# Two transpositions moved ahead of loads on the DMA queue of an attention and MLP kernel

## The chip, the cores and the metric

The kernel runs on one core of a Trainium2 chip. The metric is device time in microseconds, the median of several runs of the whole kernel. TensorE, VectorE, ScalarE and GpSimd compute; SyncE (SP in the profile) issues the DMAs.

## What is computed

The reference is a linear attention with decay, followed by an MLP with a tanh GELU. Cut to what matters:

```python
# q, k, v: (4, 8, 768, 64); lam: (8,); blocks of 64 positions
intra = einsum('bhic,bhjc->bhij', qb, kb) * Dmask        # lam ** (i - j), causal
intra = einsum('bhij,bhjd->bhid', intra, vb)
inter = einsum('bhid,bhde->bhie', qb * lam_pow, kv_state)
out[block] = intra + inter
kv_state = lam_block * kv_state + einsum('bhsd,bhse->bhde', kb * rev_pow, vb)
# then, on x of shape (3072, 512):
h = x @ w_in                                             # (512, 2048)
g = 0.5 * h * (1 + tanh(c * (h + 0.044715 * h**3)))
return g @ w_out                                         # (2048, 512)
```

## The kernel before

**Steps.** The attention is cut into 24 steps. One step is a block of 256 positions of one batch, for four of the eight heads; two steps make the 256 rows of `x` that belong to one block. For each step three loads of 256 KB are issued, q, k and v, by `load_step` (line 70). Their tiles `q32`, `k32` and `v32` come from a pool with four buffers each.

**Preparation of a step.** `prep_qk(s)` does two things. `cast_qk` makes a float16 tile `qk16` of both: VectorE multiplies q by a decay (`cast_q`, line 282), ScalarE copies k (`cast_k`, line 295). Then `transpose_dma` (line 303) has the DMA engines transpose that tile into `qkT`, for steps 8 and later; the instruction is issued by SP and waits for both casts. `scale_v` (line 266) has GpSimd scale v.

**Attention of a step.** `scores` (line 350) are TensorE's products of keys and queries, read out of `qkT`, into two PSUM banks `S`. `causal` (line 360) has VectorE multiply them by the mask into `PT`. `products` gives a step's output in two banks `OK`. From step 13 on, steps go in pairs through `burst`: all scores of two newer steps, then the outputs `O` of older steps (line 460, two banks), then the state products `K` of the newer steps (line 475, two banks), then the rest of `O` (lines 488 and 498); ScalarE copies the outputs to `xT` (lines 527 and 529).

**The MLP as filler.** The rows that the attention has finished go through the MLP in pieces, kept in a list `filler`; `fill(n)` emits the next n of them between the parts of the attention. A piece of the first product fills one PSUM bank `Hps` with four matmuls (line 613), and ScalarE applies the GELU from it (line 617). Pieces of the second product (line 692) come after these.

**PSUM.** All tiles in PSUM come from one pool of eight banks, which are handed out in turn. A tile can be written when the engine that empties the tile of eight allocations before has done so. Around the change TensorE's order of new banks is: six `Hps` (between 81.6 and 86.9 us), four `S` of steps 13 and 14, two `O`, two `K`, then `Hps` again.

**Order.** Nothing is scheduled: `pin` keeps every instruction in the order in which the program writes it, on its engine. So the order of SP's DMAs is that of the calls `load_step`, `transpose_dma` and the stores. Around the change it is, in the loop over n = 11 and 12 and after it:

```
n = 11: transposition of 13, v of 14, q and k of 16
n = 12: transposition of 14, transposition of 15, v of 15, v of 16
after:  q and k of 17, transposition of 16, v of 17, two stores
```

The matching orders on the other engines are, for ScalarE: cast of k of step 15, three GELUs, cast of k of step 16, three GELUs, copies of `O`; for VectorE: cast of q of 15, a sum of weights (line 151), cast of q of 16, the masks of steps 13 and 14. TensorE has the six `Hps`, then `burst((13, 14), (12,))`, six more `Hps`, and `burst((15, 16), (13, 14))`.

Of the kernel before, what the change touches and what calls it, by code (L numbers as in the profile page):

```python
# [15 lines left out]
def kernel(  # L16
# [43 lines left out]
    def load_step(s, names="qkv"):  # L60
        b, r = divmod(s, 2 * NSB)
        sb, half = divmod(r, 2)
        ts = ld32.setdefault(s, [])
        for nm, src in (("q", q), ("k", k), ("v", v)):
            if nm not in names:
                continue
            t = ld.tile([P, HH, 2, D], FP32, tag=nm + "32", name=f"{nm}32_{s}")
            rows = src[b, half * HH : (half + 1) * HH, sb * SB : (sb + 1) * SB, :]
            queue = nc.scalar if (nm, s) == ("v", 0) else nc.sync
            pin(queue.dma_start(out=t[:].rearrange("p h j d -> p h (j d)"),  # L70
                                in_=rows.rearrange("h (p j) d -> p h (j d)", j=2)))
            ts.append(t)
# [191 lines left out]
    def scale_v(s):  # L264
        tv = a16p.tile([P, 2, HH, D], FP16, tag="v16", name=f"v16_{s}")
        pin(nc.gpsimd.tensor_tensor(wide(tv[:]), ld32[s][2][:], decay(dv, s), ALU.mult))  # L266
        a16[s] = a16[s] + (tv,)

    def prep_qk(s):
        cast_qk(s)  # L270
        transpose_dma(s)

    def cast_qk(s):
        cast_q(s)
        cast_k(s)

    def cast_q(s):
        q32 = ld32[s][0]
        tqk = a16p.tile([P, 2, 2, HH, D], FP16, tag="qk16", name=f"qk16_{s}")
        tq, tk = tqk[:, 0], tqk[:, 1]  # L280
        q_eng = nc.gpsimd if s == 3 else nc.vector
        pin(q_eng.tensor_tensor(wide(tq), q32[:], decay(dq, s), ALU.mult))  # L282
        if s == 0:
            inverse(halves[0])
            odd(halves[1])
            inverse(halves[1])
        a16[s] = (tq, tk)
        whole_qk[s] = tqk

    def cast_k(s):  # L290
        tk, k32 = a16[s][1], ld32[s][1]
        if s == 4:
            pin(nc.vector.tensor_copy(out=wide(tk), in_=k32[:]))
        else:
            pin(nc.scalar.activation(out=wide(tk), in_=k32[:], func=AF.Copy))  # L295
# [3 lines left out]
    def transpose_dma(s):  # L299
        tqk = whole_qk.pop(s)  # L300
        if s >= FIRST_DMA_T:
            o = qkp.tile([P, 2, 2, 2, P], FP16, tag="qkT", name=f"qkT_{s}")
            pin(nc.sync.dma_start_transpose(out=o[:].rearrange("p a j h t -> p (a j h) t"),
                                            in_=tqk[:].rearrange("p a j h d -> p (a j h d)")))
            qkT[s] = o
            if s == FIRST_DMA_T + 1:
                load_step(s + 1, "v")

    def stage_t(s):
        if s >= FIRST_DMA_T:  # L310
            return
        tq, tk = a16[s][:2]
        if s < 4:
            Tps = [ps_M.tile([P, 2, 2, P], FP16, tag="M", name=f"Tps{i}") for i in range(2)]
        else:
            Tps = ps_M.tile([P, 2, 2, 2, P], FP16, tag="M", name="Tps")
        for i, t in enumerate((tq, tk)):
            to = Tps[i] if s < 4 else Tps[:, i]
            for hp in range(2):
                for j in range(2):  # L320
                    pin(nc.tensor.transpose(to[:, j, hp, :], t[:, j, 2 * hp : 2 * hp + 2, :],  # L321
                                            ident[:]))
        o = qkp.tile([P, 2, 2, 2, P], FP16, tag="qkT", name=f"qkT_{s}")
        if s < 4:
            pin(nc.scalar.activation(out=o[:, 0], in_=Tps[0][:], func=AF.Copy))
            pin(nc.vector.tensor_copy(out=o[:, 1], in_=Tps[1][:]))
        elif s in (5, 6, 8):
            pin(nc.scalar.activation(out=o[:], in_=Tps[:], func=AF.Copy))
        else:
            pin(nc.vector.tensor_copy(out=o[:], in_=Tps[:]))  # L330
        qkT[s] = o
# [203 lines left out]
    def update(s, c, parts="tu"):  # L535


        sbg, half = divmod(s, 2)
        sb = sbg % NSB
        if c == 1 and sb == NSB - 1:  # L540
            Kps.pop(s)
            return
        if "t" in parts:
            K = (Kps[s] if c == 0 else Kps.pop(s))[c].rearrange("p (hp d) -> p hp d", hp=2)
            t = ucp.tile([P, 2, D], FP32, tag=f"t{half}", name=f"t_{s}_{c}")
            if sb == 0 and c == 0:
                pin(nc.vector.tensor_copy(out=t[:], in_=K))
            else:
                for hp in range(2):
                    pin(nc.vector.scalar_tensor_tensor(  # L550
                        t[:, hp, :], state[half][:, hp, :],
                        lamu[:, 2 * half + hp : 2 * half + hp + 1], K[:, hp, :],
                        ALU.mult, ALU.add))
            state[half] = t
        if "u" in parts:
            if (s if c == 0 else s + 2) in NARROW:
                u = ubp.tile([P, 2, 2, D], FP16, tag=f"u{half}", name=f"u_{s}_{c}")[:, 0]
                pin(nc.gpsimd.tensor_tensor(  # L558
                    u, state[half][:],
                    lamu[:, 2 * half : 2 * half + 2].unsqueeze(2).to_broadcast([P, 2, D]),  # L560
                    ALU.mult))
                us[(s, c)] = u
                return
            u = ubp.tile([P, 2, 2, D], FP16, tag=f"u{half}", name=f"u_{s}_{c}")
            pin(nc.gpsimd.tensor_tensor(  # L565
                u[:], state[half][:].unsqueeze(2).to_broadcast([P, 2, 2, D]),
                lumask[:, 2 * half : 2 * half + 2, :].unsqueeze(3).to_broadcast([P, 2, 2, D]),
                ALU.mult))
            us[(s, c)] = u
# [21 lines left out]
    def store_pair(pair):  # L591
        rows = out[2 * pair * P : 2 * pair * P + 2 * P, :].rearrange("(i p) d -> p i d", p=P)
        for i in range(2):
            pin(nc.sync.dma_start(out=rows[:, i], in_=o_pairs[pair][:, i]))
# [363 lines left out]
    def fill(n):  # L958
        for _ in range(min(n, len(filler))):
            filler.pop(0)()  # L960

    def R(n, s, ahead=None, keep=False):

        def first():
            if n is not None:
                scores(n)
            if ahead:
                ahead()

        if s in NARROW:  # L970
            products(n, s, between=first)
        else:
            first()
            products(n, s)
        if n is not None:
            causal(n)
        if s is not None and s % 2 == 1:
            g, i = group_of[s // 2]
            if i == len(groups[g]) - 1 and g > 0:
                queue_group(g)  # L980
        if n is not None and not keep:
            update(n, 0)

    def U(n):
        update(n, 1)
# [98 lines left out]
    for n, (a, b, c, d) in FILL.items():  # L1084
        stage_t(n)
        fill(a + (n == 10))
        if n == 8:
            cast_q(n + 2)
            fill(1)
            cast_k(n + 2)  # L1090
            transpose_dma(n + 2)
        else:
            prep_qk(n + 2)
        if n < 11:
            load_step(n + 4, "qkv" if n < 10 else "qk")
        if n == 9:
            store_pair(1)
        if n == 11:
            scale_v(13)
            load_step(14, "v")  # L1100
            load_step(16, "qk")
        elif n == 9:
            scale_v(11)
        elif n == 10:
            scale_v(12)
            load_step(15, "qk")
        elif n == 12:
            scale_v(14)
        fill(b + (n == 8) - (n == 10))
        R(n, n - 1, keep=n == 8)  # L1110
        fill(c)
        if n == 8:
            update(n, 0)
            scale_v(n + 2)
            fill(2)
        U(n)
        if n == 12:
            prep_qk(15)
            load_step(15, "v")
            load_step(16, "v")  # L1120
            scale_v(15)
        fill(d)
        if n > 8:
            sum_win((n - 7) // 2, (n - 1) % 2, nc.vector)

    cast_qk(16)
    load_step(17, "qk")
    transpose_dma(16)
    load_step(17, "v")
    while kept_stores:  # L1130
        kept_stores.pop(0)()
    scale_v(16)
# [86 lines left out]
```

## Time and profile before

| | |
|---|---|
| median of 3 runs | 198.23 us (198.18 to 198.6) |
| the profiled execution's own time | 198.31 us |
| its span | 196.5 us |
| TensorE matmul busy | 189.7 us (97%) |
| VectorE, ScalarE, GpSimd busy | 145.7, 126.0, 68.1 us |
| DMA queue of SP | 62240 packets, 37.50 MB |
| granted TensorE clock | full nearly throughout (mean 0.997) |

The span is the time from the first to the last instruction that the profiler recorded on the core; the run's time has 1.8 us around it. Busy times are sums over instructions; a matmul's end is modelled, so TensorE's busy share does not say how near it is to its peak. In a timeline each row is a start in us, a length in us, the engine and line, the operation, the tiles, how many were merged, and in brackets the idle time ahead of it with what ended it. SPq is SP's issuing of DMAs: its rows tell when a DMA was issued, not when its data arrived. The landing comes from the DMA view, as the time from the start of the issue to the last completion mark.

### The profile page before, as it was taken

The numbers are of one execution on the slowest core, as the hardware profiler recorded it, in microseconds if no ns is written. First come the engines' busy times: TensorE is split into PE (matmuls) and PEld (weight loads), VectorE is DVE, ScalarE is ACT, GpSimd is POOL, SyncE is SP. The second block draws the span as 40 slices with busy tenths as digits, with TensorE's granted clock in tenths as the row PEclk, the third lists the DMA queues.
The fourth block names the chain that finished last, engine by engine and source line by source line (L and its number), as shares of the span: only waits on it lengthen the run. The fifth ranks groups of instructions, "written<-read, shape, count | busy, mean of one in ns | idle before, by whom it ended". The sixth has DMA issues, their size and how long they took to land.

```text
span 196.5 us, 5992 instructions
## 1 busy us (share of the span) xinstructions
PE 189.7 (97%) x2469; PEld 138.7 (71%) x2469; DVE 145.7 (74%) x291; ACT 126.0 (64%) x250; POOL 68.1 (35%) x85
## 2 busy tenths in 40 slices
PE   8878999999999999999999999999999999999992
PEld 2546544456888888654688754578888888888882
DVE  4987732889989879949889926999557996487520
ACT  3673778357774796686856379844877856678211
POOL 6594213557444732068524416064002030002000
PEclk9999999999999999999999999999999999999998
DMA  6999999999999999999997999600520300021105
GB/s 168 291 322 385 386 386 387 298 286 295 255 218 237 262 343 219 213 217 302 256 275 169 266 307 156 146 4 0 47 87 29 110 5 0 3 107 45 65 29 184
DMA packets 62810, 38.13 MB, mean 194 GB/s; under 512 B 18624, under 2 KB 55744, under 8 KB 62784
## 3 DMA queue, kind: packets, MB, share of 16 engines
q1 hardware_dynamic: 62240, 37.50, 76.8%
q8 instruction: 19, 0.31, 0.7%
q10 hardware_dynamic: 544, 0.26, 0.5%
q14 instruction: 7, 0.06, 0.1%
HBM read 27.26 MB, written 6.29 MB: 171 GB/s over the span
## 4 chain that ended last, share of the span: by engine, by line
PE 89%; SPq 4%; DMA 4%; ACT 0%; issue 0%
PE Hps L613 25%; PE MX L692 18%; PE MY L692 9%; PE HX L791 7%; PE O2ps L628 7%; PE MW L692 4%; DMA wi<-in_moe_w_in_dram 4%; SPq L70 4%; PE HY L791 4%; PE S L350 3%; PE Hps L890 3%; PE HW L791 2%; PE O L460 1%; PE OK L400 1%; PE Tps L321 1%; PE OK L422 1%
## 5 line engine op out<-in xcount | busy, mean ns | idle before, releaser
L613 PE MATMUL Hps<-xT,w_in 128*128 128x512 f16 (+1 forms) x288 | 50.5, 332 | 0.0
L613 PEld LDWEIGHTS <-w_in 128*128 128x128 f16 x288 | 27.8, 98 | 19.4
L617 ACT ACTIVATE gT<-Hps 128x512 f16<-128x512 f32 x56 | 32.6, 597 | 9.1 <-PE Hps L613 8.7
L360 DVE TENSOR_TENSOR PT<-S,mask 128x512 f16<-128x512 f32 x48 | 30.3, 680 | 8.6 <-PE S L350 8.6
L692 PEld LDWEIGHTS <-gs 128*128 128x128 f16 x320 | 31.1, 98 | 3.7
L266 POOL TENSOR_TENSOR v<-v,dv 128x512 f16<-128x512 f32 x24 | 27.5, 1150 | 17.3 <-DMA v<-in_v_dram 17.1
L692 PEld LDWEIGHTS <-gT 128*128 128x128 f16 x240 | 23.2, 98 | 3.5 <-ACT gT L617 0.2
L565 POOL TENSOR_TENSOR u<-t,lumask 128x256 f16<-128x256 f32 x21 | 15.2, 737 | 22.6 <-DVE t L550 13.6
L692 PE MATMUL MX<-w_sum,gs 128*128 128x256 f16 x160 | 21.4, 273 | 0.0
L662 DVE TENSOR_TENSOR gs<-gT 128x1024 f16<-128x1024 f16 (+1 forms) x24 | 17.2, 722 | 3.0 <-ACT gT L617 3.0
L282 DVE TENSOR_TENSOR qk<-q,dq 128x512 f16<-128x512 f32 x23 | 18.3, 798 | 1.2 <-DMA q<-in_q_dram 1.1
L295 ACT ACTIVATE qk<-k 128x512 f16<-128x512 f32 x23 | 14.4, 625 | 7.2 <-DMA k<-in_k_dram 7.1
L744 POOL TENSOR_TENSOR o<-u,q 128x512 f32<-128x512 f32 (+1 forms) x5 | 6.1, 1212 | 37.0 <-ACT u L709 37.0
L558 POOL TENSOR_TENSOR u<-t,lamu 128x128 f16<-128x128 f32 x19 | 10.7, 572 | 21.3 <-DVE t L550 15.7
L628 PE MATMUL O2ps<-w_out,gT 128*128 128x512 f16 x64 | 14.6, 379 | 0.0
L791 PEld LDWEIGHTS <-ws 128*128 128x128 f16 x128 | 12.4, 98 | 1.6 <-DVE xs L770 0.2
L529 ACT ACTIVATE xT<-OK 128x256 f16<-128x256 f32 x22 | 8.7, 453 | 6.7 <-PE OK L422 3.1
L709 ACT ACTIVATE u<-MX 128x256 f32<-128x256 f32 x18 | 6.9, 383 | 7.4 <-PE MX L692 7.4
L628 PEld LDWEIGHTS <-gT 128*128 128x128 f16 x64 | 6.1, 98 | 6.6
L692 PE MATMUL MY<-w_out,gs 128*128 128x256 f16 x80 | 10.7, 273 | 0.0
L805 DVE COPY u<-HX 128x512 f32<-128x512 f32 x8 | 5.5, 689 | 6.8 <-ACT gT L809 4.4
L692 PE MATMUL MX<-w_sum,gT 128*128 128x256 f16 x80 | 10.4, 273 | 0.0
(105 smaller groups left out, 322.0 us busy)
## 6 DMA issues: line engine op xcount, KB each, us to landing
q<-in_q_dram SPq DMA_DIRECT2D x24, 256.0 KB, 5.0
k<-in_k_dram SPq DMA_DIRECT2D x24, 256.0 KB, 5.1
v<-in_v_dram SPq DMA_DIRECT2D x23, 256.0 KB, 5.2
out_dram<-o SPq DMA_DIRECT2D x23, 256.0 KB, 4.1
wo<-in_moe_w_out_dram SPq DMA_DIRECT2D x4, 1024.0 KB, 9.5
wi<-in_moe_w_in_dram SPq DMA_DIRECT2D x4, 512.0 KB, 8.2
wi<-in_moe_w_in_dram SPq DMA_DIRECT2D x2, 1024.0 KB, 12.8
v<-in_v_dram ACTq DMA_DIRECT2D x1, 256.0 KB, 4.3
```

Of the source, the lines that this page charges most:

```text
L266: pin(nc.gpsimd.tensor_tensor(wide(tv[:]), ld32[s][2][:], decay(dv, s), ALU.mult))
L282: pin(q_eng.tensor_tensor(wide(tq), q32[:], decay(dq, s), ALU.mult))
L295: pin(nc.scalar.activation(out=wide(tk), in_=k32[:], func=AF.Copy))
L360: pin(nc.vector.tensor_tensor(t[:, hl].rearrange("p b c d -> p b (c d)"), Sps[:].rearrange("p b c d -> p b (c d)"), mask[:].unsqueeze(1).t ...
L558: pin(nc.gpsimd.tensor_tensor(u, state[half][:], lamu[:, 2 * half : 2 * half + 2].unsqueeze(2).to_broadcast([P, 2, D]), ALU.mult))
L565: pin(nc.gpsimd.tensor_tensor(u[:], state[half][:].unsqueeze(2).to_broadcast([P, 2, 2, D]), lumask[:, 2 * half : 2 * half + 2, :].unsqueez ...
L613: pin(nc.tensor.matmul(by_block(Hps[:, i, :]), w_in16[:, c, f * P : (f + 1) * P], x(c), start=(c == 0), stop=(c == NC - 1)))
L617: pin(nc.scalar.activation(out=dst, in_=Hps[:], func=AF.Gelu_apprx_tanh))
L628: pin(nc.tensor.matmul(O2[tau][0][:], gT[:, f % HF, f // HF, tau * P : (tau + 1) * P], w_out16[:, f, :], start=(n == 0), stop=(n == NF - 1)))
L662: pin(nc.vector.tensor_tensor(g_rows(m, i), g_rows(a, i), g_rows(b, i), op))
L692: pin(nc.tensor.matmul(dst, lhsT, rhs, start=(opens and i == 0), stop=(closes and i == HF - 1), skip_group_check=True))
L791: pin(nc.tensor.matmul(dst[:, i, :], w_in_block(a, slice(c, c + 1), slice(f * P, f * P + P))[:, 0], x_block(b, slice(c, c + 1))[:, 0], sta ...
```

## The change

At two places a transposition is issued ahead of two loads that stood ahead of it. The loads of q and k of step 16 go from n = 11 to n = 12, behind the transposition of step 14. The loads of q and k of step 17 go behind the transposition of step 16; there the separate calls become `prep_qk(16)` and `load_step(17)`, which issue the same instructions. The number of instructions does not change, nor does the order on TensorE, VectorE, ScalarE and GpSimd, nor the PSUM banks.

```diff
             prep_qk(n + 2)
         if n < 11:
             load_step(n + 4, "qkv" if n < 10 else "qk")
+        elif n == 12:
+            load_step(16, "qk")
         if n == 9:
             store_pair(1)
         if n == 11:
             scale_v(13)
             load_step(14, "v")
-            load_step(16, "qk")
         elif n == 9:
             scale_v(11)
...
-    cast_qk(16)
-    load_step(17, "qk")
-    transpose_dma(16)
-    load_step(17, "v")
+    prep_qk(16)
+    load_step(17)
     while kept_stores:
         kept_stores.pop(0)()
     scale_v(16)
```

SP's order after the change:

```
n = 11: transposition of 13, v of 14
n = 12: transposition of 14, q and k of 16, transposition of 15, v of 15, v of 16
after:  transposition of 16, q, k and v of 17, two stores
```

## Prediction

> **What bounds the kernel now.** I read the page first. Its chain of work that ended last is nearly all TensorE:
>
> ```profile
> PE 89%; SPq 4%; DMA 4%; ACT 0%; issue 0%
> ```
>
> From about 20 us to 193 us the chain is TensorE without a break, so an earlier transfer gains only where TensorE waited for it, and any new TensorE wait goes whole into the end. The change sits between 80 and 94 us. The chain there, in order of time (start, us, what):
>
> ```profile
> 81.80 5.18 PE Hps L613 x24
> 86.98 0.67 PE S L350 x32
> 87.88 0.28 PE K L475 x32
> ...
> 93.56 0.57 PE S L350 x32
> ```
>
> These are the two bursts: scores of steps 13 and 14 at 86.98, of 15 and 16 at 93.56. The same 32 matmuls take 0.67 us in the first and 0.57 in the second. So at most 0.10 us at step 14's scores can be a wait for its transposition. That is all the first move can give back.
>
> The order in time on the DMA queue (SP: start, us to issue):
>
> ```profile
> 79.47 0.58 SPq L70 DMA_DIRECT2D v<-in_v_dram  x1
> 80.10 0.51 SPq L70 DMA_DIRECT2D q<-in_q_dram  x1
> 80.65 0.55 SPq L70 DMA_DIRECT2D k<-in_k_dram  x1
> 81.36 3.32 SPq L303 DMA_TRANSPOSE qkT<-qk  x2
> 84.73 1.93 SPq L70 DMA_DIRECT2D v<-in_v_dram  x2
> 86.71 0.51 SPq L70 DMA_DIRECT2D q<-in_q_dram  x1
> 87.26 0.51 SPq L70 DMA_DIRECT2D k<-in_k_dram  x1
> 87.93 1.85 SPq L303 DMA_TRANSPOSE qkT<-qk  x1
> ```
>
> 80.10 and 80.65 are q and k of step 16, 81.36 the transpositions of 14 and 15, 86.71 and 87.26 q and k of step 17, 87.93 the transposition of 16. Asked for the loads issued from 80.65, the DMA view gives the landing:
>
> ```profile
> k<-in_k_dram SPq DMA_DIRECT2D x1, 256.0 KB, 4.4
> ```
>
> 80.65 + 4.4 is 85.0. Who takes it, in the timelines of VectorE, ScalarE and TensorE:
>
> ```profile
> 84.18 0.86 DVE L282 TENSOR_TENSOR qk<-q,dq 128x512 f16<-128x512 f32 x1 [0.59 <-DMA q<-in_q_dram]
> ```
> ```profile
> 84.43 0.60 ACT L617 ACTIVATE gT<-Hps 128x512 f16<-128x512 f32 x1 [0.27 <-PE Hps L613]
> 85.03 0.63 ACT L295 ACTIVATE qk<-k 128x512 f16<-128x512 f32 x1
> 85.57 1.19 ACT L617 ACTIVATE gT<-Hps 128x512 f16<-128x512 f32 x2
> 87.02 0.60 ACT L617 ACTIVATE gT<-Hps 128x512 f16<-128x512 f32 x1 [0.27 <-PE Hps L613]
> ```
> ```profile
> 87.48 0.39 PE L460 MATMUL O<-PT,v 64*64 64x128 f16 x16
> 87.71 0.45 PE L475 MATMUL K<-v,qk 64*64 64x64 f16 x32
> ```
>
> VectorE already waits 0.59 us for q of step 16. ScalarE takes k of step 16 at 85.03, in the very moment it lands: no slack. Behind it stand three GELUs. PSUM's eight banks go round in order of allocation, so the second `O` bank needs the fourth `Hps` bank of this run emptied, the first `K` bank the fifth, the second `K` bank the sixth. The sixth GELU ends at 87.02 + 0.60 = 87.62, TensorE wants that bank at about 87.73: slack 0.1 us.
>
> [...] The trace agrees with the order: v of 14 lands 3.8 us after 79.47, at 83.3, q of 16 at 84.2, k at 85.0. [...] The trace has one such packet at 85.25, 996 ns long, on the instruction queue.
>
> That fetch matters. The windows (us; five engines busy; clock, DMA share, GB/s) show full flow, then almost none:
>
> ```profile
> 81.25:85.50 4.25, 4.25 (x24) 2.09 (x22) 3.07 (x7) 3.50 (x8) 2.07 (x2) 1.00 1.25 295
> 85.75:87.00 1.25, 1.25 (x12) 0.47 (x14) 0.00 (x0) 0.99 (x2) 0.81 (x2) 1.00 0.05 6
> ```
>
> [...] The semaphore of the DMA just ahead of that transposition is held too: the transposition of 14 finished its packets by 85.5, yet fifteen of its sixteen marks came at 87.10 to 87.19. The same happened one fetch earlier: k of 15, issued at 75.33, took 6.2 us, where k of 16 took 4.4.
>
> **The change part by part.** No instruction is added or removed. The engines' own orders, their waits for PSUM and the banks stay; SP's order alone changes, at two places.
>
> Transposition of 14 ahead of q and k of 16. On SP it goes past two loads (0.51 + 0.55 us). Its casts were done by 79.8 (VectorE: 79.08 + 0.68), so it can start at 80.10 instead of 81.36 and lands near 84.2. Gain at TensorE: at most 0.10 us, and that only brings TensorE sooner to banks that ScalarE has not emptied; I take 0.
>
> q and k of 16 slip behind it: on SP by its issue time, 1.7 us (half of 3.32), in the DMA engines by 256 KB, 0.9 us at 295 GB/s. The flow is full, so the 0.9 counts first: k of 16 ends its packets where the transposition of 14 did, about 85.4 instead of 84.4, directly ahead of the transposition of 15. Lower bound of its landing L: 85.03 + 0.9 = 85.9. If held as its predecessor in that place was: 87.1. I take 87.1, since fetch, place and following transposition are the same.
>
> What waits: ScalarE stands at the cast from 85.03 to L. Then cast to next GELU 0.54 (85.57 - 85.03), two GELUs 1.19, the last 0.59: the sixth bank is free at L + 2.32, and with 0.06 for the signal TensorE's second `K` bank starts at L + 2.38 instead of 87.73. TensorE's new wait is **L - 85.35**. With 87.1 it is 1.75 us, with 85.9 0.55. It begins at the `O` matmuls (87.48) and all later TensorE work follows behind it, with no idle time to take it up. VectorE's cast of q, at worst 87.2 to 88.0, delays step 13's mask by 0.6; its result is first read in the next burst, at 94: nothing.
>
> Transposition of 16 ahead of q and k of 17. It needs the cast of k of 16: 87.1 + 0.63 = 87.7, so it issues near 87.8, as before (87.93), and lands near 92.5; step 16's scores come at 93.8 + 1.75. Gain 0. q and k of 17 go out near 89.7 and 90.2, 3 us later, and land near 93.9 and 94.7. Their casts stood at 92.53 (VectorE) and 94.09 (ScalarE). Behind the first is the mask of step 15, whose scores now come after 95.3; behind the second the copies of `O`, now near 96.9. Both covered by 0.5 us or more; if that cover fails, a few tenths. v of 17 and the stores follow about 1 us late, covered by the 1.75.
>
> Sum: own time of the profiled execution 198.31 (span 196.5 and 1.8 around it) + 1.75 = 200.06. The median of the runs is 0.08 below that execution: **200.0**.
>
> **The rivals.**
> 1. Forecast, k of 16 held by the stopped transposition of 15: 200.0. Chance 0.55.
> 2. k of 16 is only 0.9 us later, not held[...]. For it: the packets of k end near 85.4. Against it: k of 15. 198.23 + 0.55 = 198.8. Chance 0.23.
> 3. SP's issue of the transposition is long, as the 3.43 us of step 13's at 76.00: then q goes out at 83.6, k at 84.2, which lands 3.4 to 4.4 later, 87.6 to 88.6: 200.5 to 201.4. Chance 0.07.
> 4. Not slower: the loads do not pay for the transposition, because DMA time is regained ahead of them at the stop of 79.75 to 81 us and k of 16 lands by 85.35. That is the deciding point. TensorE then keeps the 0.10: 198.1. Against it: the flow behind that stop is full to 85.5. Chance 0.15, of which 0.06 for a gain beyond 0.2%, through an order of fetch and transposition that I don't see. That the change does not do what it says is excluded by SP's order.
>
> **How the numbers follow.** 0.2%, 0.4 us, is about what a measurement of this kernel can tell from no change. Slower: 0.55 + 0.23 + 0.07 = 0.85; same 0.09, faster 0.06. The range takes in cases 1 and 2 and the edge of 3: 198.7 to 200.5; given case 1 alone it is 199.6 to 200.3.
>
> **What would show it.** Right: ScalarE idle 1 to 2 us ahead of the cast at 85, ended by the DMA of k; a TensorE gap of that size at 87.5 to 89, at the `O` or `K` matmuls; the scores of 15 and 16 late by as much; the scores of 13 and 14 in 0.57. Wrong: k of 16 cast before 85.4 and no gap at 87.7; or a gap elsewhere, as at the scores of 15 and 16.

## The result, and the profile after

The changed kernel takes 200.54 us in the median of six runs (200.22 to 202.49), the kernel before in the same runs 198.34 us. The ratio is 1.0128, with a 95% interval of 1.0088 to 1.0168: slower by 2.2 us in the medians. Ratios here and below are worked out together with their intervals and differ a little from the quotient of two medians (1.0111 here). A single run more than 1.5% above the fastest of its kernel counts in the median and not in the ratio; there are two, one of 203.09 us with the first move alone and one of 201.46 us with k ahead of q. The forecast was 200.0 us in a range of 198.7 to 200.5: the sign and the place were right, the size was too small, and the median lies just above the range's upper end. The profiled execution itself took 200.22 us, with a span of 198.4 us, 1.9 us longer than before.

The page's chain, by engine, answers to the line that was shown first of before. ScalarE's share has come up from 0 to 2%, that of DMAs from 4 to 7%:

```profile
PE 85%; DMA 7%; SPq 5%; ACT 2%; issue 1%
```

The same chain of the changed kernel in order of time (start, us, what) names the place:

```profile
82.63 5.04 DMA k<-in_k_dram
87.67 0.02 issue
87.69 0.63 ACT qk L295
88.32 1.47 ACT gT L617 x3
89.79 0.04 issue
89.83 0.44 PE K L475 x31
```

So TensorE's part of the chain, unbroken in this place before, is broken by the load of k of step 16, its cast, and three GELUs. SP's issues in the changed kernel show the new order, the transposition of 14 at 80.50, q and k of 16 behind it, the transposition of 16 at 88.34:

```profile
80.50 1.46 SPq L303 DMA_TRANSPOSE qkT<-qk  x1
82.00 0.58 SPq L70 DMA_DIRECT2D q<-in_q_dram  x1
82.63 0.51 SPq L70 DMA_DIRECT2D k<-in_k_dram  x1
83.29 1.24 SPq L303 DMA_TRANSPOSE qkT<-qk  x1
84.58 1.14 SPq L70 DMA_DIRECT2D v<-in_v_dram  x2
88.34 1.24 SPq L303 DMA_TRANSPOSE qkT<-qk  x1
```

ScalarE's timeline: the cast that had no idle time ahead of it has 2.56 us, and the GELUs behind it follow back to back from 88.23 us, though the last `Hps` matmul that they read had ended at 87.09:

```profile
84.53 0.60 ACT L617 ACTIVATE gT<-Hps 128x512 f16<-128x512 f32 x1 [0.27 <-PE Hps L613]
87.69 0.63 ACT L295 ACTIVATE qk<-k 128x512 f16<-128x512 f32 x1 [2.56 <-DMA k<-in_k_dram]
88.23 1.55 ACT L617 ACTIVATE gT<-Hps 128x512 f16<-128x512 f32 x3
```

TensorE's timeline: it stops at the second `O` matmul, and again at the first and second `K` matmul, each until a GELU has emptied its bank. At the first `K` the row names no wait, since the modelled end of the `O` matmuls covers it; the second GELU ends at 89.29 and this matmul starts at 89.34.

```profile
87.02 0.64 PE L350 MATMUL S<-qkT 64*64 64x128 f16 x32
87.49 0.22 PE L460 MATMUL O<-PT,v 64*64 64x128 f16 x1
88.86 0.41 PE L460 MATMUL O<-PT,v 64*64 64x128 f16 x15 [1.15 <-ACT gT L617]
89.34 0.19 PE L475 MATMUL K<-v,qk 64*64 64x64 f16 x1
89.83 0.44 PE L475 MATMUL K<-v,qk 64*64 64x64 f16 x31 [0.30 <-ACT gT L617]
```

Two rows of the same timeline before, for comparison:

```profile
86.91 0.74 PE L350 MATMUL S<-qkT 64*64 64x128 f16 x32
88.21 5.34 PE L613 MATMUL Hps<-xT,w_in 128*128 128x512 f16 x24
```

The scores at 87.02 take 0.64 us, where before they took 0.74: the wait of step 14's scores did go, and TensorE reached the next wait that much sooner.

The windows of the changed kernel (us; five engines busy; clock, DMA share, GB/s) show the stop of DMA traffic again, now at 86.25 to 87.5:

```profile
81.25:85.50 4.25, 4.25 (x25) 2.19 (x23) 2.47 (x7) 3.13 (x7) 1.79 (x3) 1.00 1.13 278
86.25:87.50 1.25, 1.25 (x37) 0.68 (x36) 0.02 (x1) 0.00 (x0) 0.61 (x2) 1.00 0.12 8
```

### The profile page after: what moved, and what is told of

It is laid out like the page before. It is cut to its first block, busy times and chain, and to the rows that moved or that the text cites. A ratio compares the mean times of both kernels' runs of the same rounds, so it can differ in the third digit from the quotient of the medians.

```text
span 198.4 us, 5992 instructions
## 1 busy us (share of the span) xinstructions
PE 190.6 (96%) x2467; PEld 139.2 (70%) x2469; DVE 145.3 (73%) x291; ACT 125.5 (63%) x250; POOL 67.0 (34%) x85
## 4 chain that ended last, share of the span: by engine, by line
PE 85%; DMA 7%; SPq 5%; ACT 2%; issue 1%
PE Hps L613 22%; PE MX L692 17%; PE MY L692 9%; PE HX L791 7%; PE O2ps L628 7%; PE MW L692 4%; DMA wi<-in_moe_w_in_dram 4%; SPq L70 4%; PE HY L791 4%; PE Hps L890 3%; PE S L350 3%; DMA k<-in_k_dram 3%; PE HW L791 2%; PE OK L400 1%; PE O L460 1%; PE Tps L321 1%
## 5 line engine op out<-in xcount | busy, mean ns | idle before, releaser
L565 POOL TENSOR_TENSOR u<-t,lumask 128x256 f16<-128x256 f32 x21 | 15.7, 760 | 21.8 <-DVE t L550 12.7
L744 POOL TENSOR_TENSOR o<-u,q 128x512 f32<-128x512 f32 (+1 forms) x5 | 5.6, 1124 | 37.0 <-ACT u L709 37.0
L558 POOL TENSOR_TENSOR u<-t,lamu 128x128 f16<-128x128 f32 x19 | 9.4, 503 | 21.5 <-DVE t L550 15.8
L350 PEld LDWEIGHTS <-qkT 64*64 64x64 f16 x384 | 6.3, 106 | 5.9 <-issue 2.3
```

The lines of the kernel that those rows point to most:

```text
L350: pin(nc.tensor.matmul(Sps[hl][half64(c), hp, jk, :], o[half64(hl), 1, jk, hp, half64(c)], o[half64(hl), 0, :, hp, half64(c)], start=True, ...
L565: pin(nc.gpsimd.tensor_tensor(u[:], state[half][:].unsqueeze(2).to_broadcast([P, 2, 2, D]), lumask[:, 2 * half : 2 * half + 2, :].unsqueez ...
```

## Experiments

The fetch, here and below, is the packet of 16 KB on the instruction queue near 85 us (from 85.58 to 86.74 us in the changed kernel). The theory: k of 16 lands late because it has slid behind a transposition and stands directly ahead of the next one, at the stop of DMA traffic behind the fetch (8 GB/s from 86.25 to 87.5 us); ScalarE's cast then holds three GELUs, and TensorE waits for their banks. Rivals: the second move carries part of the loss; the loads are simply late, wherever they stand; the runs near 202 us have another cause. All timed comparisons are with the kernel before on the same chip.

| kernel | median, us | ratio to before, 95% interval |
|---|---|---|
| changed kernel again | 200.42 | 1.0111 (1.0070 to 1.0152) |
| first move only | 201.26 (200.63 of the five runs in the ratio) | 1.0108 (1.0067 to 1.0149) |
| second move only | 198.42 | 0.9997 (0.9980 to 1.0014) |
| both moves, late cast | 198.5; again 198.4 | 0.9997 (0.9982 to 1.0012); 0.9996 (0.9981 to 1.0010) |
| two loads put between | 199.64 | 1.0048 (1.0032 to 1.0064) |
| fetch shifted | 201.16 | 1.0129 (1.0097 to 1.0161) |
| TensorE kept busy | 200.02 | 1.0077 (1.0058 to 1.0096) |
| k ahead of q | 198.82 | 1.0023 (1.0012 to 1.0034) |
| first move, late cast | 198.1; again 198.12 | 0.9989 (0.9972 to 1.0006); 0.9983 (0.9970 to 0.9995) |

**The changed kernel again**, unaltered.

> The changed kernel unaltered, for a second profile and more times. Theory (k of step 16 lands late, held by the transposition of step 15 behind it, and ScalarE's cast holds three GELUs): the cast again starts 2 to 3 us after 85 us, TensorE stands 1.5 to 2.5 us at the O and K matmuls near 88 us, 200.2 to 200.8 us. If the extra 0.3 to 0.5 us over the forecast was chance of the first runs: 199.8 to 200.2.

Measured: 200.42 us in six runs from 199.81 to 202.34. In this profile the cast starts at 88.17 us, 0.48 us later than in the first one. The loss is not chance, but its size differs from run to run, and the cast starts a little later than the 87 to 88 us that were expected. This execution took 202.34 us, and TensorE's timeline shows a second part of the loss behind the wait:

```profile
90.31 0.51 PE L475 MATMUL K<-v,qk 64*64 64x64 f16 x31 [0.30 <-ACT gT L617]
90.75 0.40 PE L498 MATMUL O<-qkT,u 128*128 128x128 f16 x2
90.94 6.84 PE L613 MATMUL Hps<-xT,w_in 128*128 128x512 f16 x24
97.71 0.64 PE L350 MATMUL S<-qkT 64*64 64x128 f16 x32
```

The 24 `Hps` matmuls take 6.84 us here and 5.34 in the kernel before. From the second `K` bank to the next scores it is 97.71 - 90.31 = 7.40 us here, and 95.60 - 89.83 = 5.77 in the changed kernel's first profile: 1.63 us more, of the 2.12 by which the two executions differ. The windows of this run show a lower clock there (it is the number after POOL's busy time):

```profile
87.13:90.54 3.41, 1.55 (x79) 1.11 (x80) 2.48 (x4) 2.37 (x5) 0.40 (x1) 1.00 0.94 221
90.55:93.95 3.40, 3.40 (x36) 1.41 (x22) 1.44 (x7) 1.11 (x3) 3.06 (x6) 0.50 0.85 212
```

The granted clock was 0.50 from 90.55 to 93.95 us. In the 3.41 us before, TensorE was busy for 1.55 us, at a clock of 1.00.

**The first move alone.**

```diff
-    prep_qk(16)
-    load_step(17)
+    cast_qk(16)
+    load_step(17, "qk")
+    transpose_dma(16)
+    load_step(17, "v")
```

> Only the transposition of step 14 is moved. Theory: the whole loss is here: 200.2 to 200.8 us, the same gap at the O and K matmuls. Rival (the second move carries part of it, through q and k of step 17 issued 3 us later): 199.7 to 200.1 us.

Measured: ratio 1.0108 against 1.0111 for both moves beside it. The whole loss is in the first move. Its profile is of the longest execution, 203.09 us. ScalarE's and TensorE's rows there are:

```profile
88.99 0.63 ACT L295 ACTIVATE qk<-k 128x512 f16<-128x512 f32 x1 [3.52 <-DMA k<-in_k_dram]
90.15 0.41 PE L460 MATMUL O<-PT,v 64*64 64x128 f16 x15 [2.12 <-ACT gT L617]
```

TensorE was busy for 0.96 us of the 3.40 from 87.68 to 91.08 us, at a granted clock of 1.00; from 91.09 to 94.49 us the clock was 0.50.

**The second move alone.** The loads of step 17 go behind the transposition of 16, and the rest stays as before.

> Only the transposition of step 16 is moved. Theory: nothing changes, 198.2 to 198.5 us; the transposition of step 16 issues at about 86.7 instead of 87.9 us and its result waits for TensorE. Rival (the second move carries part of the loss): 198.7 us or more.

Measured: 198.42 us, ratio 0.9997. The transposition of 16 issued as soon as v of 16 was out and landed at 91.63 us, over two microseconds ahead of the burst that uses it (its scores start at 94.29): no gain and no loss.

**Both moves, with the cast of k of 16 behind the three GELUs.** `fill(3)` is what emits these GELUs; the edit is against the changed kernel, cut to what matters.

```diff
-    prep_qk(16)
-    load_step(17)
+    cast_q(16)
...
     fill(3)
+    cast_k(16)
+    transpose_dma(16)
+    load_step(17)
```

> The changed order on the DMA queue, with the cast of k of step 16 put behind the next three GELUs on ScalarE (and the transposition of step 16 after it). Theory (the loss is the three GELUs behind a cast that waits): TensorE's gap at the O and K matmuls goes, the scores of steps 13 and 14 take 0.57 us, 198.1 to 198.4 us. Rival (the loss comes from elsewhere in the new order, as late q and k of step 17, or a late transposition of step 16): 199 us or more, with a gap at another place.

Measured: 198.5 us, ratio 0.9997. The load was as late as ever, the cast started at 88.26 us, and TensorE had no gap at `O` and `K`:

```profile
87.39 0.39 PE L460 MATMUL O<-PT,v 64*64 64x128 f16 x16
87.62 0.50 PE L475 MATMUL K<-v,qk 64*64 64x64 f16 x32
```

So the loss was the order on ScalarE's queue together with the late load, and not the late load alone. One thing had not been expected: a gap of 0.69 us at the matmuls after the *second* burst, as TensorE's timeline of this kernel shows:

```profile
94.70 0.41 PE L488 MATMUL O<-qkT,u 64*64 64x128 f16 x12
95.80 1.89 PE L613 MATMUL Hps<-xT,w_in 128*128 128x512 f16 x8 [0.69 <-DVE PT L360]
```

VectorE there waits 1.08 us for q of step 17, which the second move sends later; its mask of step 15, behind that cast, frees the bank late.

**v of 15 and 16 between k of 16 and the next transposition.**

```diff
-            prep_qk(15)
+            cast_qk(15)
             load_step(15, "v")
             load_step(16, "v")
+            transpose_dma(15)
```

> The changed order, but the transposition of step 15 goes behind v of 15 and 16, so that k of step 16 no longer stands directly ahead of a transposition. Theory A (the mark of the DMA directly ahead of a stopped transposition is held): k of 16 lands at 86.0 to 86.4 us, TensorE's gap at the O and K matmuls is 0.5 to 1.0 us, about 199.0 us, no half-clock window. Rival B (the load itself is late[...]): k lands at 87.0 us or later and the gap stays over 1.5 us, 200 us.

Measured: 199.64 us, ratio 1.0048, between the two expectations: about half of the loss went. The profile is of the longest of its 12 executions (201.59 us). In it fifteen of the sixteen marks of k came at 86.57 to 86.67 us and the last at 88.25, and ScalarE waited for that one:

```profile
88.27 0.63 ACT L295 ACTIVATE qk<-k 128x512 f16<-128x512 f32 x1 [2.73 <-DMA k<-in_k_dram]
```

So the fifteen are no longer held, as theory A has it, and one mark is late by itself, 1.58 us behind them, which puts the landing where rival B has it. Both are seen in this execution, and the second is what the theory lacked. Why that mark is late, and how late it is in the other eleven, where the loss is smaller, no trace shows.

**The fetch shifted by 64 TensorE instructions.**

```diff
-    idle(2, 512)
+    idle(34, 512, 16)   # 34 matmuls of 16 columns in place of 2 of 512
```

> The changed kernel with 64 more TensorE instructions at the start (32 narrow matmuls and their weight loads in place of two wide idle ones, while TensorE waits for the first weights), so that [...] the fetch of 85.6 us moves to about 81 us. Theory (this fetch stops the transposition of 15 and holds k of 16): the stop ahead of k of 16 goes, k lands at 85.9 to 86.5 us, gap 0.5 to 1.0 us, about 199.0 us. Rival (the stop has nothing to do with the fetch, or the fetch is not TensorE's): k still at 87.5 us or later, 200.2 us or more.

Measured: 201.16 us. The time and the landing are in the rival's range, but its reason is not borne out, and the theory's forecast is not either: the fetch moved from 85.58 only to 84.36 us, and the stop moved with it, to 84.75 to 86 us, as the windows of this kernel show:

```profile
83.50:84.75 1.25, 1.25 (x8) 0.56 (x6) 1.12 (x5) 1.16 (x3) 0.00 (x0) 1.00 1.28 294
84.75:86.00 1.25, 1.25 (x8) 0.54 (x7) 0.59 (x1) 0.90 (x2) 1.20 (x1) 1.00 1.67 19
86.00:87.00 1.00, 1.00 (x6) 0.47 (x5) 0.00 (x0) 0.60 (x1) 1.00 (x3) 1.00 0.93 216
```

The transposition of 14 landed behind this stop, at 86.99 us, and k of 16 behind it at 88.78. The time can't be read for the shift alone. At the start of this execution a load of k landed at 13.95 us (12.83 before) and TensorE waited 1.04 us for its cast. Behind that wait, at 15.14 us, 16 matmuls of line 400 took 0.57 us in the chain, at 21.07 us 0.35; the mean clock of the execution is 0.990.

**TensorE kept busy through its wait**: the scores of step 14 done six times over.

```diff
-        for hp in range(2):
+        for hp in list(range(2)) * (6 if n == 14 else 1):
```

> The changed kernel with the score matmuls of step 14 done six times over the same values (80 more matmuls, 1.4 us), so that TensorE is busy through most of its wait. Theory [...]: no run at a mean clock near 0.99, all runs within 199.6 to 200.8 us, median about 200.2 us. Rival (the slow tail comes from the loads landing later still in those runs): the tail to 202 us stays, or the median rises by the 1.4 us of added matmuls to 201.8 us.

The theory was that the runs near 202 us are those with a stretch at half clock behind the wait, as the second profile has (0.50 from 90.55 to 93.95 us). Measured: 200.02 us, six runs from 199.73 to 200.53, none with a mean clock below 0.997. With 80 more matmuls the kernel is not slower than the changed one but quicker in the median (1.0077 against 1.0111 and 1.0128, with intervals that overlap), and none of the six runs is near 202 us. ScalarE still idled 2.35 us for k. So the wait costs about 1.7 us by itself. That the runs near 202 us are made by the clock is read from their records: the three of the changed kernel have a mean clock of 0.989 to 0.991, the other nine 0.997 or more. That the added matmuls removed them is likely and not settled by six runs, as nine of twelve were free of it without them. With the 160 added instructions (matmuls and weight loads, all TensorE's) this trace has 20 fetches in place of 19, and the one after 85.3 us came at 90.5 instead of 98.0: more instructions of TensorE brought it sooner.

**k of 16 issued ahead of q of 16.**

```diff
-            load_step(16, "qk")
+            load_step(16, "kq")   # the same two loads, k first
```

> The changed kernel with k of step 16 issued ahead of q of step 16. Theory (whichever DMA stands directly ahead of the transposition of 15 lands last, near 87.5 us, and ScalarE's wait for k is what costs): k lands at 85.2 to 85.9 us and ScalarE idles at most 0.9 us; q lands at 87 us or later, VectorE's cast of it and the masks of step 13 behind it are about 1 us late, and TensorE's gap moves to the first Hps matmuls after the burst, which need the score banks of step 13: 198.8 to 199.6 us. Rival (both loads are late alike[...]): gap still at the O and K matmuls, 200.2 us or more.

Measured: 198.82 us, ratio 1.0023. k landed at 85.41 and q, now directly ahead of the transposition of 15, at 87.78 us. ScalarE did not idle for k; VectorE idled for q, and TensorE at the first `Hps` after the burst:

```profile
85.58 0.62 ACT L295 ACTIVATE qk<-k 128x512 f16<-128x512 f32 x1
87.81 0.69 DVE L282 TENSOR_TENSOR qk<-q,dq 128x512 f16<-128x512 f32 x1 [2.71 <-DMA q<-in_q_dram]
89.15 5.34 PE L613 MATMUL Hps<-xT,w_in 128*128 128x512 f16 x24 [0.17 <-DVE PT L360]
```

The median met the forecast's lower end. Exchanging two loads took away four fifths of the loss: what matters is which engine waits for the DMA in that place.

**The first move kept, the second undone, the late cast.** The edit is against the changed kernel, whose `prep_qk(16)` and `load_step(17)` go.

```diff
+    cast_q(16)
+    load_step(17, "qk")
...
     fill(3)
+    cast_k(16)
+    transpose_dma(16)
+    load_step(17, "v")
```

> The first move kept, the second undone (q and k of step 17 ahead of the transposition of 16), and the cast of k of 16 behind the next three GELUs on ScalarE. Theory: neither burst waits for a load, the mask of step 15 is not late as it was in the run with the late cast alone (gap 0.9 us after the second burst), 198.0 to 198.4 us, at or up to 0.2 us under the kernel before. Rival (the transposition of 16, behind both, is late for the second burst): a gap at the scores of step 16, 198.8 us or more.

Measured: 198.1 us, ratio 0.9989 with an interval that just includes 1. It was repeated with more runs beside the late cast with both moves:

> First move kept, second undone, late cast; repeated beside the next. Theory: 198.0 to 198.2 us, 0.1 to 0.3 us under the kernel before. Rival (the gain of the first trial was chance): equal to the kernel before within 0.1 us.

Measured: 198.12 us in 22 runs, the kernel before 198.49 in 59; ratio 0.9983 (0.9970 to 0.9995). This version is quicker than the kernel before by some 0.3 us (0.1 to 0.6 by the interval), and than the changed kernel by over 2 us. The late cast without either move was not tried, so how much of the 0.3 us is the first move's is open; at its scores the row has 0.64 us in place of 0.74. In its profile k of 16 landed at 87.61 us, as late as in the changed kernel, and TensorE's rows run through:

```profile
86.95 0.64 PE L350 MATMUL S<-qkT 64*64 64x128 f16 x32
87.42 0.39 PE L460 MATMUL O<-PT,v 64*64 64x128 f16 x16
87.64 0.50 PE L475 MATMUL K<-v,qk 64*64 64x64 f16 x32
88.08 0.28 PE L498 MATMUL O<-qkT,u 128*128 128x128 f16 x2
88.20 5.34 PE L613 MATMUL Hps<-xT,w_in 128*128 128x512 f16 x24
```

> Both moves with the late cast, repeated beside the version with the second move undone. Theory (with TensorE's wait gone the second move costs something, since q of step 17 then lands too late for VectorE's order): slower than that version by 0.2 to 0.6 us in the median. Rival (the second move costs nothing): the same within 0.1 us.

Measured: 198.4 us, 0.28 us above the version with the second move undone, with the gap after the second burst again, 0.41 us ahead of 95.53. The medians fit the theory, but the two intervals overlap, so a cost of the second move is likely and not settled.

## Why the prediction was right and wrong

- **What bounds, and the gain of the first move (0): right.** The 0.10 us at step 14's scores came back and was spent waiting for banks.
- **The path of the loss: right.** Late k, the cast first in ScalarE's queue, three GELUs, the `O` and `K` banks: each link is in the chain or the timelines of the changed kernel, and the late cast removes the loss.
- **The landing L: mis-sized.** This is the step that failed. It was put at 87.1 us, from the single stop in the trace of before, "since fetch, place and following transposition are the same". It was 87.67 in the first profile (0.46 more, as that run is 0.11 us late already at 87.0), 88.15 in the second, and 88.97 with the first move alone. Place and transposition were the same; the fetch was not. Its packet ran from 85.58 to 86.74 us in the first profile, where in the trace of before it ran from 85.25 to 86.25: 0.49 us, and 0.09 more since the last mark there came at 87.19 and not 87.10. In these two traces the last of the held marks came 0.93 and 0.94 us after the end of this packet (87.67 - 86.74 and 87.19 - 86.25); why it did, no trace shows. L differed by 0.48 us between two executions of the same kernel, so one execution gives one draw of it.
- **From L to the second `K` bank: a little too long.** It was put at 2.38 us. Measured: 89.83 - 87.67 = 2.16, since GELUs with their inputs ready run back to back, three in 1.55 us, not 1.19 + 0.59. This took back 0.2 us of the error in L, which is luck.
- **TensorE's new wait**: put at 1.75 us, measured 89.83 - 87.84 = 1.99 (87.84 is 87.73 plus the 0.11). The profiled execution, 200.22 us, is 0.16 us above the 200.06 that the sum gave for it. That execution is the quickest of its six. The sum took the median to lie 0.08 us below the profiled execution, as before; it lay 0.32 us above, and this is the larger part of the miss.
- **A term was missing: the clock.** In the second profile the wait (1.49 us at `O`, 0.30 at `K`) was followed by 3.4 us at half clock. In 3 of the 12 runs of the changed kernel the mean clock was 0.989 to 0.991, and these took 202.2 to 202.5 us, where the other nine took 199.8 to 201.2, with a median of 200.41. That is about 1.9 us more in a quarter of the runs, of which 1.63 us is the clock in the one with a trace; the median of the twelve rises by 0.1 us through it. The rest of the spread is likely the landing, 0.48 us later in the second profile than in the first; the other ten runs have no trace. A mean clock of 0.991 also stands in one of the 27 runs of the kernel before that were taken beside the first experiments (198.96 us), so a mean clock as low came without this wait.
- **The second move (0): right as it stands**, 0.9997 alone. The warning that its cover could fail was borne out where TensorE's wait was taken away.
- **The held marks: half of it.** Putting loads between, and exchanging q and k, show that place ahead of the transposition matters. That one mark of the sixteen alone can be late, by 1.58 us in the run with loads between, was not in the reasoning. What stays open is whether the fetch makes the stop: that the two moved together was seen (84.36 us for 85.58, and 84.75 for 86.25), but no run without a fetch was tried.

The third rival, a long issue of the moved transposition, did not happen: it took 1.46 us. The fourth, DMA time regained ahead of the loads, did not either.

## What to carry to other kernels

A DMA that is moved ahead pays with those it passes: find who takes each of them, with what idle time ahead of the taking, and what stands behind it in that engine's queue. A cast with no idle time in front, and with three GELUs behind it that empty TensorE's banks, is a wait of TensorE that has not happened yet; putting the cast behind these GELUs cost nothing with the first move alone and took the loss away, though the load stayed late. When a forecast rests on a landing, take its spread from several executions, look at where the instruction fetch stands in each, and look at the granted clock behind a long wait (0.50 for 3.4 us here in two of the traces).

## What the runs showed of the hardware

- The granted clock was 0.50 from 90.55 to 93.95 us in the changed kernel's second profile, behind a wait in which TensorE was busy for 1.55 us between 87.13 and 90.54, and from 91.09 to 94.49 us with the first move alone, behind one with 0.96 us between 87.68 and 91.08. It stayed at 1.00 in the changed kernel's first profile, with 2.99 us between 84.71 and 88.13 and 2.31 us between 88.13 and 91.54, and with loads between, with 2.09 us between 86.23 and 89.64. What sets it these runs do not show. The executions of the two profiles of the changed kernel took 202.34 and 200.22 us.
- In three traces DMA traffic fell for 1.25 us behind the start of the fetch: to 6 GB/s from 85.75 to 87 us before (fetch at 85.25 us; 295 and 296 GB/s in the windows on both sides), to 8 GB/s from 86.25 to 87.5 us in the changed kernel (fetch at 85.58; 278 and 282), to 19 GB/s from 84.75 to 86 us with the fetch shifted (fetch at 84.36; 294 and 216). The transposition of step 15 was the next of SP's DMAs behind the held one in the first two.
